# Sparse attention and a gated feed-forward layer on one core: all engines in source order to the end of block one, heads on even and odd partitions, half products in front

## The chip, the core and the metric

The kernel runs on one core of one Trainium2 chip. The metric is the device time of one execution in microseconds (us); less is better. A core has PE (matrix products), DVE (vector work), ACT (activations and copies), POOL (general work) and SP, whose queue issues all of this kernel's transfers. Each engine works through its own queue in order and waits for semaphores of the others.

## What is computed

For 8 batches of 576 tokens and 8 heads of 64, each head attends sparsely: heads 0 to 3 to the last 32 positions, heads 4 to 7 to the earlier positions that agree modulo 32. The 4608 x 512 result goes through a feed-forward layer with 2048 hidden columns.

```python
mask_local = (rel >= 0) & (rel < stride)
mask_strided = (rel >= 0) & (pos[None, :] % stride == pos[:, None] % stride)
...
attn = np.exp(scores)
attn = attn / (np.sum(attn, axis=-1, keepdims=True) + 1e-09)
return np.matmul(attn, v).astype(np.float32)
...
h = x @ w_in
g = h * (1.0 / (1.0 + np.exp(-h)))
return (g @ w_out).astype(np.float32)
```

## The kernel before

**Attention.** A batch is six groups: three local ones of 12 tiles, three strided ones of 8, 8 and 6. A group covers pairs of heads. It runs through these steps:

- scores (L265): the keys of both heads lie block-diagonally in a buffer kbd, and one product per tile gives both heads' scores in a PSUM bank pss
- peaks (L278, DVE, one per part of 64 columns): scores plus mask, and the row's peak
- exp, in two forms. In batch 0 ("early") POOL subtracts the whole group from its peaks (L290), ACT takes one exp (L291), DVE sums (L292). In later batches ACT takes one exp with a sum per part (L284)
- reciprocal of the sum (L295, L296); strided groups are multiplied by it on DVE (L299)
- transposes (L307) and a copy pt (L309); values (L316 local, L336 strided); local results are scaled (L322), transposed back (L328) and copied into xb (L331), strided ones are copied there into strided places (L349)

Loads of kbd and vbd (values) write 64 partitions per transfer, one half of the partitions for each head of a pair (L226 to L237). Three buffers of each serve batch 0, two serve the later batches.

**Feed-forward.** Tokens go in nine blocks of 512, hidden columns in 16 steps of 128. A step is `hidden` (L372: twelve products of 512 columns, three for each of the four 128-row parts of x, because x and the weights are split into a high and a low part), the silu (L393 tanh on ACT, L394 on DVE, L354 high part ghi on DVE, L355 low part glo, on POOL in block one and on DVE later), and `output` (L401, twelve products) one step behind. The x parts xhi and xlo come from L354 (ACT) and L355 (DVE).

**Weights.** The weights are loaded once, in 32 pieces that come as 64-bit numbers through six staging buffers. A piece costs two activations on ACT (L164, L169) and three operations on DVE (L172, L176, L177). `weights(2 * fc + 3)` splits up to piece 2*fc+2 ahead of step fc of block one.

**Order.** `between` runs after each `hidden` and each `output` of a block, 32 times ("halves"), and does the next piece of a later batch's attention at set halves (`due_at`). Only from the first product on, and only on PE, is the order the source's (L534). Everything else, and PE up to there, is ordered by a scheduler that goes by its own times. Loads up to the end of batch 0's attention are chained in the order of `FIRST` (L50: k and v are loads of a group, p of a piece), and the first piece's split is held behind the last exp of batch 0 (`marks`, L512).

Of the kernel before, what the change touches and what calls it, by code (L numbers as in the profile page):

```python
# [17 lines left out]
PSUM = bass.MemoryType.PSUM  # L18

B, H, S, D = 8, 8, 576, 64  # L20
DM, DFF = 512, 2048
STRIDE = 32
# [27 lines left out]
FIRST = "k0 k1 k2 v0 k3 v1 k4 k5 v2 p0 p1 v3 v4 v5 p2 p3 k6 k7 v6 p4 p5"  # L50
# [29 lines left out]
def sparse_attention_ffn(ctx: ExitStack, tc: tile.TileContext, kqt, vt, w_in, w_out, out):  # L80
# [8 lines left out]

    ident = const.tile([P, P], F32, name="ident")  # L90
    make_identity(nc, ident)
# [7 lines left out]
    def keep(m, p0, rows, shape, steps, base, channel):  # L99
# [6 lines left out]


    lent = {
        (1, 0, 12): "stage0", (1, 0, 14): "stage1", (1, 1, 12): "stage2", (1, 1, 14): "stage3",
        (1, 0, 9): "vbd2", (1, 1, 9): "zeros", (1, 0, 7): "kbd2",  # L110
    }

    kbds = [const.tile([P, 3, QW], F32, name=f"kbd{i}") for i in range(KBUFS + 1)]
    vbds = [const.tile([P, 2, VT * D], F32, name=f"vbd{i}") for i in range(VBUFS + 1)]
    zeros = const.tile([P, VT * D], F32, name="zeros")
    nc.vector.memset(zeros, 0.0)
    for kbd in kbds:
        nc.vector.memset(kbd[D:P, 0], 0.0)  # L120
        nc.vector.memset(kbd[0:D, 2], 0.0)
    for vbd in vbds:
        nc.scalar.copy(out=vbd[D:P, 0], in_=zeros[D:P])
        nc.scalar.copy(out=vbd[0:D, 1], in_=zeros[0:D])
    vbds = [vbd.rearrange("p h (t d) -> p h t d", d=D) for vbd in vbds]

# [6 lines left out]
    for starts in sorted({s for g in GROUPS for s in g.starts if s}):  # L133
        first = const.tile([P, 72], F32, name="mask_first" + "".join(map(str, starts)))
        nc.vector.tensor_copy(out=first, in_=m)
        for t in starts:
            keep(first, t * STRIDE, STRIDE, [KW], [1], -STRIDE, 0)
        masks[True, starts] = first
    m = mask("mask_strided")
# [39 lines left out]
    queue = []  # L179
    last = {}  # L180
    marks = []
    ordered = True

    def load(out, in_):

        if not ordered:
            nc.sync.dma_start(out=out, in_=in_)
        elif queue:
            with tc.issue_after(queue[-1]):
                queue.append(nc.sync.dma_start(out=out, in_=in_).ins)  # L190
        else:
            queue.append(nc.sync.dma_start(out=out, in_=in_).ins)
# [33 lines left out]
    def load_qk(b, gi):  # L226
        n = max(GROUPS[gi].nq, GROUPS[gi].nk)
        for h in range(2):
            rows = slice(h * D, (h + 1) * D)
            load(out=kbds[gi % (KBUFS if b else KBUFS + 1)][rows, h : h + 2, :n],  # L230
                 in_=kqt[b, gi, rows, :, :n])

    def load_v(b, gi):
        n = GROUPS[gi].count
        for h in range(2):
            rows = slice(h * KW, (h + 1) * KW)
            load(out=vbds[gi % (VBUFS if b else VBUFS + 1)][rows, h, :n], in_=vt[b, gi, rows, :n])  # L237
# [8 lines left out]
    def attention(gi, b, early):  # L246

        g = GROUPS[gi]

        def bank(name):  # L250

            if early and name != "pss":
# [3 lines left out]
        kbd = kbds[gi % (KBUFS + 1 if early else KBUFS)]  # L256
        vbd = vbds[gi % (VBUFS + 1 if early else VBUFS)]
        cols = g.n * P
        tiles = [(t, t // g.per, slice(t % g.per * g.rows, (t % g.per + 1) * g.rows))
                 for t in range(g.count)]  # L260

        pss = bank("pss")
        s_ps = pss.rearrange("p (c h k) -> p c h k", h=2, k=KW)
        for t, c, rows in tiles:
            nc.tensor.matmul(  # L265
                s_ps[rows, c], kbd[:, 1, g.q0[t] : g.q0[t] + g.rows],
                kbd[:, 0:3:2, g.k0[t] : g.k0[t] + KW], start=True, stop=True,
            )
        yield

        sm = att.tile([P, 512], F32, name="sm")
# [348 lines left out]
```

## Time and profile before

| | us |
|---|---|
| three runs | 983.05, 984.2, 986.59 |
| median | 984.2 |
| the profiled execution | 985.2 |
| its span | 983.4 |
| PE busy in the span | 943.8 |
| PE busy before 76.33 us | 43.2 |

The profile shows one execution. A row of its timeline gives the start, the length, the engine, the line of the kernel, the operation with what it writes and reads, and in brackets how long the engine stood idle before it and what released it. PE's busy time overlaps (the next product starts before the last has drained), so rates are taken from the distance between starts.

### The profile page before, as it was taken

Reading aid. Unit: us, or ns where it says so; the run is one execution under the profiler, and the core shown is the slowest. Engines: PE = TensorE matmul, PEld = TensorE weight load, DVE = VectorE, ACT = ScalarE, POOL = GpSimd, SP = SyncE. Lnnn points to the kernel's source line nnn. Section 1 sums busy time; section 2 is a strip of 40 time slices with the busy share of each in tenths; the row PEclk is TensorE's granted clock in tenths of the full one; section 3 lists DMA queues with packets and bytes.
Section 4 is the critical chain, followed back from the end, with each engine's and each line's share of the span. In section 5 each row is a group of like instructions: output and inputs, shape, how many; then the busy total and the mean of one; then the engine's idle time right before and its main releaser. Section 6 shows DMA issues by size and latency. Waiting matters only on the chain.

```text
span 983.4 us, 15231 instructions
## 1 busy us (share of the span) xinstructions
PE 943.8 (96%) x5896; PEld 749.5 (76%) x5896; DVE 421.1 (43%) x1384; ACT 323.6 (33%) x988; POOL 37.0 (4%) x44
## 2 busy tenths in 40 slices
PE   5559999999999999999999999999999999999998
PEld 3447877778777877787777877787778878888886
DVE  5986733344354334433434344343433333334232
ACT  4865524224242323333423233232422231012011
POOL 3022122000000000000000000000000000000000
PEclk9769999999999999999999999999999999999999
DMA  9974411201131023111211113011210010001001
GB/s 229 279 266 145 147 38 52 90 25 45 50 97 36 26 53 95 44 37 44 77 57 43 44 35 106 26 45 51 86 36 20 1 44 1 1 0 43 1 1 43
DMA packets 36488, 62.86 MB, mean 64 GB/s; under 512 B 4161, under 2 KB 23617, under 8 KB 36417
## 3 DMA queue, kind: packets, MB, share of 16 engines
q1 hardware_dynamic: 36416, 61.90, 21.5%
q8 instruction: 46, 0.75, 0.3%
q14 instruction: 26, 0.20, 0.1%
HBM read 52.45 MB, written 9.44 MB: 63 GB/s over the span
## 4 chain that ended last, share of the span: by engine, by line
PE 91%; DMA 4%; DVE 2%; ACT 1%; POOL 1%; issue 0%; SPq 0%; ACTq 0%; POOLq 0%
PE po L405 41%; PE ps L377 40%; PE ps L265 4%; PE ps L336 2%; DMA stage<-w_out 2%; PE ps L316 2%; PE ps L307 2%; DMA stage<-w_in 1%; POOL glo L355 1%; PE ps L328 1%; DVE stage L172 1%; DMA vbd<-vt 1%; ACT sm L284 0%; ACT stage L164 0%; DMA kbd<-kqt 0%
## 5 line engine op out<-in xcount | busy, mean ns | idle before, releaser
L377 PE MATMUL ps<-xhi,w 128*128 128x512 f32 x1152 | 391.6, 400 | 7.1 <-ACT xhi L354 7.1
L394 DVE SCALAR_TENSOR_TENSOR th<-th,ps 128x512 f32<-128x512 f32 (+1 forms) x147 | 99.3, 676 | 424.4 <-ACT th L393 423.9
L377 PEld LDWEIGHTS ps<-xhi,w 128*128 128x128 f32 x1152 | 217.7, 189 | 63.7 <-ACT xhi L354 7.7
L393 ACT ACTIVATE th<-ps 128x512 f32<-128x512 f32 (+1 forms) x147 | 86.4, 588 | 495.7 <-PE ps L377 491.7
L377 PE MATMUL ps<-xlo,w 128*128 128x512 f32 x576 | 228.2, 396 | 1.3 <-DVE xlo L355 1.3
L405 PE MATMUL po<-w,ghi 128*128 128x512 f32 x576 | 189.8, 401 | 0.7 <-DVE ghi L354 0.7
L405 PEld LDWEIGHTS po<-w,ghi 128*128 128x128 f32 x576 | 107.4, 189 | 28.8 <-issue 4.2
L377 PEld LDWEIGHTS ps<-xlo,w 128*128 128x128 f32 x576 | 109.2, 190 | 26.4 <-DVE xlo L355 2.5
L405 PE MATMUL po<-w,glo 128*128 128x512 f32 x252 | 100.6, 399 | 4.5 <-POOL glo L355 4.5
L284 ACT ACTIVATE sm<-sm,nmax 128x64 f32<-128x64 f32 x280 | 93.8, 337 | 31.2 <-DVE nmax L278 31.2
L355 DVE TENSOR_TENSOR glo<-th,ghi 128x512 fp32r<-128x512 f32 (+1 forms) x131 | 89.0, 679 | 8.9 <-DVE ghi L354 0.5
L405 PE MATMUL po<-stage,ghi 128*128 128x512 f32 x288 | 90.9, 397 | 0.0
L354 DVE CAST ghi<-th 128x512 fp32r<-128x512 f32 (+1 forms) x147 | 61.8, 420 | 9.0 <-DVE th L394 0.5
L405 PEld LDWEIGHTS po<-stage,ghi 128*128 128x128 f32 x288 | 53.6, 188 | 12.7
L405 PEld LDWEIGHTS po<-w,glo 128*128 128x128 f32 x252 | 47.8, 190 | 16.7 <-POOL glo L355 5.4
L405 PE MATMUL po<-stage,glo 128*128 128x512 f32 x144 | 56.8, 395 | 0.0
L265 PE MATMUL ps<-kbd 128*32 128x128 f32 (+1 forms) x928 | 47.7, 289 | 8.5 <-DMA kbd<-kqt 8.5
L284 ACT ACTIVATION_READ_ACCUMULATOR sm<-sm,nmax 128x1 f32 x280 | 52.8, 189 | 0.0
L265 PEld LDWEIGHTS ps<-kbd 128*32 128x32 f32 (+1 forms) x928 | 35.1, 125 | 16.9 <-issue 16.2
L405 PE MATMUL po<-vbd,ghi 128*128 128x512 f32 x108 | 43.9, 407 | 0.0
L405 PE MATMUL po<-vbd,glo 128*128 128x512 f32 x108 | 42.4, 392 | 0.0
L405 PE MATMUL po<-zeros,ghi 128*128 128x512 f32 x108 | 42.1, 390 | 0.0
(75 smaller groups left out, 740.0 us busy)
## 6 DMA issues: line engine op xcount, KB each, us to landing
vbd<-vt SPq DMA_DIRECT2D x48, 192.0 KB, 3.3
out<-osb SPq DMA_DIRECT2D x36, 256.0 KB, 2.1
stage<-w_in SPq DMA_DIRECT2D x16, 512.0 KB, 5.9
stage<-w_out SPq DMA_DIRECT2D x16, 512.0 KB, 4.2
kbd<-kqt SPq DMA_DIRECT2D x32, 221.0 KB, 3.6
kbd<-kqt SPq DMA_DIRECT2D x32, 208.0 KB, 3.4
vbd<-vt SPq DMA_DIRECT2D x32, 128.0 KB, 2.7
kbd<-kqt SPq DMA_DIRECT2D x16, 224.0 KB, 3.6
```

The source lines that it names most:

```text
L172: nc.vector.scalar_tensor_tensor(out=upper, in0=upper, scalar=3, in1=lower, op0=ALU.logical_shift_left, op1=ALU.bitwise_or,)
L265: nc.tensor.matmul(s_ps[rows, c], kbd[:, 1, g.q0[t] : g.q0[t] + g.rows], kbd[:, 0:3:2, g.k0[t] : g.k0[t] + KW], start=True, stop=True,)
L284: last["act"] = nc.scalar.activation(out=s_sb[:, c, h], in_=s_sb[:, c, h], func=AF.Exp, bias=nmax[:, c, h : h + 1], scale=-1.0, accum_out= ...
L307: nc.tensor.transpose(psp[:, at], sm[:, at], ident)
L316: nc.tensor.matmul(o_ps[rows, c], pt[:, c * P + rows.start : c * P + rows.stop], vbd[:, :, t], start=True, stop=True,)
L336: last["pe"] = nc.tensor.matmul(pso[h * D : (h + 1) * D, t * SEQ : (t + 1) * SEQ], vbd[:, h, t], pt[:, p0 : p0 + SEQ], start=True, stop=True,)
L354: copy(out=hi, in_=src)
L355: sub(out=lo, in0=src, in1=hi.bitcast(F32))
L377: nc.tensor.matmul(ph, weight(0, wi, fc)[:, cc * P : (cc + 1) * P], x[xi][:, cc], start=n == 0, stop=n == 3 * NP - 1,)
L393: nc.scalar.activation(out=th[:, cols], in_=ph[:, cols], func=AF.Tanh, scale=0.5)
L394: nc.vector.scalar_tensor_tensor(out=th[:, cols], in0=th[:, cols], scalar=1.0, in1=ph[:, cols], op0=ALU.add, op1=ALU.mult,)
L405: nc.tensor.matmul(po[tt], g[gi][:, cols], weight(1, wi, fc), start=fc == 0 and n == 0, stop=fc == NFC - 1 and n == 2,)
```

## The change

- **Source order.** PE is in source order from the start, and ACT, DVE, POOL and SP are too until block one ends (`others.close()`). The chained loads, `marks` and `issue_after` go. Blocks two to nine are scheduled as before.
- **The prologue written out.** A loop over eight steps s does: peaks of group s, values of s-2, sum and transposes of s-1, scores of s+1, transposes back of s-2. Weight piece 0 is split at s = 5, behind the peaks and the exp of the last group; the high and low parts of x for the first two of its four parts follow at once, and the sum of group 4 comes behind them.
- **Half products.** At s = 6 the products of steps 0 and 1 over the first half of x run, the second of them behind piece 1. Block one's first two steps run only the other half.
- **Even and odd partitions.** The two heads of a pair lie on even and odd partitions in kbd and vbd. A load writes every second partition (`h::2`) instead of 64 in a row. Scores read the keys of both heads in turn (`"p h k -> p k h"`), so in pss and sm the heads alternate by column.
- **Start.** Memsets clear whole buffers, so each first load waits for its buffer's memset; two value buffers are cleared by ACT in four copies.
- **Batch 1 ("quick", b < 2).** Its exp takes batch 0's form, so POOL and DVE have the subtraction and the sum in block one; the strided groups' multiplication is POOL's in both batches. Batch 1's groups come at halves 5, 10, 14, 19, 23, 28 instead of 1, 6, 12, 17, 22, 28, and the next scores and peaks two halves later, instead of three. A group's sum stands one half behind its peaks; for the pairs of halves 0 and 1, 2 and 3, 12 and 13, 16 and 17, 30 and 31 that is within one step, with no piece and no silu between.
- **glo** is DVE's in block one too.

```diff
-FIRST = "k0 k1 k2 v0 k3 v1 k4 k5 v2 p0 p1 v3 v4 v5 p2 p3 k6 k7 v6 p4 p5"
+FIRST = "k0 k1 v0 k2 k3 v1 k4 v2 k5 p0 v3 v4 v5 p1 p2 p3 p4 k6 v6 p5 k7"
...
+    ctx.enter_context(tc.manual_schedule(engines={PE}))
+    others = ctx.enter_context(ExitStack())
+    others.enter_context(tc.manual_schedule(engines=OTHERS))
+    nc.vector.memset(kbds[0][:, 0], 0.0)
+    nc.gpsimd.memset(kbds[0][:, 2], 0.0)
+    nc.vector.memset(kbds[1][:, 0:3:2], 0.0)
+    nc.vector.memset(vbds[0], 0.0)
+    nc.vector.memset(zeros, 0.0)
+    nc.vector.memset(kbds[2][:, 0:3:2], 0.0)
...
-            load(out=kbds[gi % (KBUFS if b else KBUFS + 1)][rows, h : h + 2, :n],
-                 in_=kqt[b, gi, rows, :, :n])
+            load(out=kbds[gi % (KBUFS if b else KBUFS + 1)][h::2, h : h + 2, :n],
+                 in_=kqt[b, gi, h::2, :, :n])
...
-                kbd[:, 0:3:2, g.k0[t] : g.k0[t] + KW], start=True, stop=True,
+                    kbd[:, 0:3:2, g.k0[t] : g.k0[t] + KW].rearrange("p h k -> p k h"),
+                    start=True, stop=True,
...
-            last["dve"] = nc.vector.tensor_mul(s_sb[:, : g.n], s_sb[:, : g.n], inv)
+                (nc.gpsimd if self.quick else nc.vector).tensor_mul(s_sb, s_sb, self.inv)
...
-        sub = nc.vector.tensor_sub if k else nc.gpsimd.tensor_sub
...
+    load_due()
+    scores(0)
+    x = new_x()
+    half_done = {}
+    early = range(NP // 2)
+    late = range(NP // 2, NP)
+    for s in range(NG + 2):
+        if s < NG:
+            groups[s].peak()
+        if s == NG - 1:
+            weights(1)
+            split_x(0, x, early)
+        if 2 <= s:
+            values(s - 2)
+        if 1 <= s <= NG:
+            groups[s - 1].total()
+            groups[s - 1].turn()
+        if s + 1 <= NG:
+            scores(s + 1)
+        if 2 <= s:
+            groups[s - 2].back()
+        if s == NG:
+            half_done[0] = hidden(0, x, early)
+            weights(2)
+            split_x(0, x, [NP // 2])
+            half_done[1] = hidden(1, x, early)
+    split_x(0, x, late[1:])
...
+        plan[at(gi)] += [(groups[c - 1].back if c > NG else None), functools.partial(values, c)]
...
+                plan[then] += [functools.partial(scores, c + n), groups[c + n].peak]
+                plan[then + 1].insert(0, groups[c + n].total)
+    plan[0] += [groups[NG].peak]
+    plan[1] += [groups[NG].total]
...
+            if k == 0 and fc in half_done:
+                ph = hidden(fc, x, late, half_done[fc])
```

ACT's queue in the second half of batch 0's attention; stage is a weight piece's staging buffer, sm and pt are a group's scores and their transposed copy. Before:

```order
L309 COPY pt<-po 128x384
L164 ACTIVATE stage_224<-stage_224 128x512
L169 ACTIVATE stage_224<-stage_224 128x512
L331 COPY xb<-po 128x384
L354 CAST xhi<-xb 128x512
L291 ACTIVATE sm<-sm 128x512
L164 ACTIVATE stage_352<-stage_352 128x512
L169 ACTIVATE stage_352<-stage_352 128x512
L309 COPY pt<-po 128x512
```

And now:

```order
L318 COPY pt<-po 128x384
L362 COPY xb<-po 128x384
L301 ACTIVATE sm<-sm 128x512
L318 COPY pt<-po 128x512
L362 COPY xb<-po 128x384
L301 ACTIVATE sm<-sm 128x384
L174 ACTIVATE stage_242<-stage_242 128x512
L179 ACTIVATE stage_242<-stage_242 128x512
L365 CAST xhi<-xb 128x512 x2
```

The first piece has moved behind the last group's exp, and x's parts behind it.

PE at the end of the first two products' early part, where the last values of batch 0 stand between the halves. Now:

```order
L389 MATMUL ps<-xhi,w_0_423 128x512
L389 MATMUL ps<-xlo,w_0_423 128x512
L389 MATMUL ps<-xhi,w_0_424 128x512
L337 MATMUL po<-pt,vbd_81 64x54 x12
L389 MATMUL ps<-xhi,w_0_423 128x512
L389 MATMUL ps<-xlo,w_0_423 128x512
L389 MATMUL ps<-xhi,w_0_424 128x512
```

Before, at the corresponding place, the last values stood inside the first product alone, and a group of batch 1's values followed soon:

```order
L336 MATMUL po<-pt,vbd_86 64x54 x12
L377 MATMUL ps<-xhi,w_0_580 128x512
L377 MATMUL ps<-xlo,w_0_580 128x512
L377 MATMUL ps<-xhi,w_0_581 128x512
L377 MATMUL ps<-xhi,w_0_580 128x512
L377 MATMUL ps<-xlo,w_0_580 128x512
L377 MATMUL ps<-xhi,w_0_581 128x512
L316 MATMUL ps<-vbd_84,pt 32x128 x12
```

Twelve products, six of each of the two steps, now stand ahead of those values; batch 1's first values have moved behind the second output group.

POOL's last rows; sm<-nmax,sm is the subtraction, sm<-sm,rsum the multiplication. Before:

```order
L290 TENSOR_TENSOR sm<-nmax,sm 128x384 x3
L290 TENSOR_TENSOR sm<-nmax,sm 128x512 x2
L290 TENSOR_TENSOR sm<-nmax,sm 128x384
L355 TENSOR_TENSOR glo<-th,ghi 128x512 x16
L616 UNCONDITIONAL_BRANCH
```

And now, from the multiplication of group 3 on:

```order
L310 TENSOR_TENSOR sm<-sm,rsum 128x4x2x64
L299 TENSOR_TENSOR sm<-nmax,sm 128x3x2x64
L310 TENSOR_TENSOR sm<-sm,rsum 128x4x2x64
L310 TENSOR_TENSOR sm<-sm,rsum 128x3x2x64
L299 TENSOR_TENSOR sm<-nmax,sm 128x3x2x64 x3
L299 TENSOR_TENSOR sm<-nmax,sm 128x4x2x64
L310 TENSOR_TENSOR sm<-sm,rsum 128x4x2x64
L299 TENSOR_TENSOR sm<-nmax,sm 128x4x2x64
L310 TENSOR_TENSOR sm<-sm,rsum 128x4x2x64
L299 TENSOR_TENSOR sm<-nmax,sm 128x3x2x64
```

The sixteen glo are gone, and the subtractions of batch 1 and six multiplications have come.

More of the change, by code (lines that the diff above doesn't have):

```diff
@@ L104, in keep @@
         )
[L108 to L125, printed above, removed]
     masks = {}
@@ L177, in split_weights @@
         nc.vector.tensor_sub(out=lo, in0=value, in1=hi.bitcast(F32))
[L179 to L192, printed above, removed]
+    load = nc.sync.dma_start
     pieces = [(0, 0)]
@@ L498, in sparse_attention_ffn @@
-    work = attention_steps()
-    def attend(groups):
-        while len(weighed) < min(groups, NG * B):
-            next(work)
     ready = 0
```

395 lines of the change are left out of this document (194 added, 201 removed).

## The prediction

> **What bounds the kernel now.** I read the page first, then the windows of PE either side of 76.33 us, the waits of PE behind that point, and last the timeline in front of it. On the page: PE's total, its busy tenths, the clock.
>
> ```profile
> PE 943.8 (96%) x5896; PEld 749.5 (76%) x5896; DVE 421.1 (43%) x1384; ACT 323.6 (33%) x988; POOL 37.0 (4%) x44
> PE   5559999999999999999999999999999999999998
> PEclk9769999999999999999999999999999999999999
> ```
>
> The windows of PE (start:end, length, busy, count, clock, DMA share, GB/s) and its waits after 76 us:
>
> ```profile
> 0.00:76.33 76.33, 43.23 (x456) 0.80 0.87 249
> 76.33:984.00 907.67, 900.58 (x5445) 1.00 0.16 48
> PE po L405 <- POOL glo L355: 1.4, 2, 0.7
> PE po L405 <- DVE ghi L354: 0.6, 1, 0.6
> ```
>
> From 76.33 us on, PE waits 2.0 us in 907 and has its full clock: that part is matmul work, and an order of other engines cannot shorten it by more than those 2.0. In front of it PE is busy 43.2 of 76.3 us at a clock of 0.80. 76.33 is where the second group of output products begins; I use it as the meeting point of both kernels. The timeline in front of it (start, us, engine, line, what; idle before and its releaser):
>
> ```profile
> 5.05 1.51 PE L265 MATMUL ps<-kbd 128*32 128x128 f32 x24 [5.05 <-DMA kbd<-kqt]
> 23.73 0.65 ACT L164 ACTIVATE stage<-stage 128x512 f32<-128x512 f32 x1 [3.06 <-DMA stage<-w_in]
> 27.86 1.09 PE L307 MATMUL po<-ident,sm 128*128 128x128 f32 x4 [6.23 <-DVE sm L299]
> 38.84 1.75 PE L336 MATMUL po<-pt,vbd 128*64 128x54 f32 x32 [4.72 <-ACT pt L309]
> 52.42 0.65 ACT L164 ACTIVATE stage<-stage 128x512 f32<-128x512 f32 x1 [2.46 <-DMA stage<-w_out]
> 54.17 0.79 PE L377 MATMUL ps<-xhi,w 128*128 128x512 f32 x1 [6.38 <-ACT xhi L354]
> 62.58 4.47 POOL L355 TENSOR_TENSOR glo<-th,ghi 128x512 fp32r<-128x512 f32 x1 [31.27 <-DVE ghi L354]
> 67.10 0.80 PE L405 MATMUL po<-w,glo 128*128 128x512 f32 x1 [3.81 <-POOL glo L355]
> 76.33 0.73 PE L405 MATMUL po<-w,ghi 128*128 128x512 f32 x2
> ```
>
> The four long PE waits have one pattern. Weight pieces stand in ACT's and DVE's queues ahead of what PE needs: ACT stops at 20.67 for a piece that lands at 23.7, the attention's copies and the last x parts queue behind, and PE pays 6.23, 4.72 and 6.38 us. The fourth, 3.81, is a 4.47 us subtraction on POOL.
>
> **The change, part by part.** Its own length per step comes from these rows of before.
>
> ```profile
> 6.74 0.23 DVE L278 CUSTOM_DVE_ANT_0 sm<-ps,mask_first 128x64 f32<-128x64 f32 x1 [1.46 <-PE ps L265]
> 7.61 0.08 DVE L278 DVE_READ_ACCUMULATOR2_ANT nmax<- 128x1 f32 x1
> 7.85 0.83 POOL L290 TENSOR_TENSOR sm<-nmax,sm 128x384 f32<-128x384 f32 x1 [2.01 <-DVE nmax L278]
> 8.71 0.52 ACT L291 ACTIVATE sm<-sm 128x384 f32<-128x384 f32 x1 [1.65 <-POOL sm L290]
> 9.72 0.55 PE L307 MATMUL po<-ident,sm 128*128 128x128 f32 x3
> 11.03 0.46 ACT L309 COPY pt<-po 128x384 f32<-128x384 f32 x1
> 14.34 1.28 PE L316 MATMUL po<-vbd,pt 128*32 128x128 f32 x24
> 15.69 0.56 DVE L322 TENSOR_TENSOR xq<-po,rsum 128x384 f32<-128x384 f32 x1 [2.82 <-PE po L316]
> 18.04 1.05 POOL L290 TENSOR_TENSOR sm<-nmax,sm 128x512 f32<-128x512 f32 x1 [4.47 <-DVE rsum L295]
> 20.73 0.68 DVE L292 TENSOR_REDUCE rsum<-sm 128x8 f32<-128x512 f32 x1
> 68.71 0.69 ACT L164 ACTIVATE stage<-stage 128x512 f32<-128x512 f32 x1
> 69.30 0.68 ACT L169 ACTIVATE stage<-stage 128x512 int32<-128x512 uint32 x1
> 71.10 0.63 PE L405 MATMUL po<-w,glo 128*128 128x512 f32 x1
> 71.53 0.68 DVE L177 TENSOR_TENSOR zeros<-stage,vbd 128x512 fp32r<-128x512 f32 x1
> 72.13 0.68 DVE L172 SCALAR_TENSOR_TENSOR stage<-stage 128x512 int32<-128x512 int32 x1
> 72.74 0.41 DVE L176 CAST w<-stage 128x512 fp32r<-128x512 f32 x1
> 71.53 0.63 PE L377 MATMUL ps<-xhi,w 128*128 128x512 f32 x1
> 75.53 0.86 PE L265 MATMUL ps<-kbd 128*32 128x128 f32 x24
> 99.78 0.39 PE L377 MATMUL ps<-xhi,w 128*128 128x512 f32 x1
> 102.57 0.49 PE L328 MATMUL ps<-ident,xq 128*128 128x128 f32 x3
> ```
>
> Read as lengths: a group's peaks 0.95 us for six parts (6.74 to 7.69), 1.25 for eight; subtraction on POOL 0.83 or 1.05; exp 0.52; sum with its two small followers about 1.05; a weight piece 1.15 on ACT (0.59 to the next start and a like second half) and 1.6 on DVE (0.60, 0.61, 0.41); twelve warm 512-column products 2.79 (99.78 to 102.57), cold ones 0.43 each (71.10 to 71.53). A handover between engines costs about 0.1 (7.69 to 7.85 is 0.16, 8.68 to 8.71 is 0.03).
>
> *Stretch A, to the end of batch zero's last scores.* The first loads now wait for a memset of their whole buffer, about 0.7 us, so the first scores start at 5.7 instead of 5.05. No weight piece stands between the groups any more. The first ring takes 4.0 us (peaks 0.95, subtraction 0.83, exp 0.52, transposes 0.55, scores 0.86, handovers 0.3), a later local one 3.2 (peaks 0.95, values 1.28 beside subtraction and exp, transposes 0.55, scores 0.9, less what overlaps): scores end at 7.2, 11.2, 14.4, 17.6. The strided groups close a longer ring: peaks 1.25, subtraction 1.05, the multiplication that moves from DVE to POOL 1.05 (by the subtraction of the same size), transposes 0.55, scores 1.1, handovers and a wait for values 1.3: 6.3. The last scores end near 24. The load of the first piece lies behind some 4.3 MB; at the 249 GB/s of the window row that lands near 20, and it is read only after the last exp, near 26. Piece one stands on SP behind the sixth group's values, whose buffer is free near 18.5; by the same rate it lands near 26 and is read at 37. So the even and odd partitions, whatever they do to a load, save nothing here.
>
> *Stretch B, to the first half product.* Here the change puts work on the path that before had done early: peaks 0.95, subtraction 0.83, exp 0.52, piece zero 1.15 and 1.6, two low parts of x 1.2, then the sum 1.05 that in source order waits behind them, multiplication 1.05, transposes 0.55, scores 1.0, values 1.1, transposes 0.4, nine handovers 0.9: 12.3 us. The half products begin at 36.3; before, the first product's last quarter waited for its x until 54.17.
>
> *Stretch C, to the second output group.* Six cold products 2.6 (38.9); the second six wait for piece one, at about 39.0 by ACT and DVE, and end at 41.6; values 0.9, their copy 0.8, the last x part 1.2 (44.6), and the late half of the first product ends near 45.7. Then the path is: piece two's 1.6 on DVE up to 46.7, the silu's three operations 1.6 (48.3), peaks 0.95, subtraction and exp with handovers 1.65 (50.9), transposes 0.4, scores 0.9 (52.2), output 2.8, product 2.8: 57.8. In source order the next transposes stand ahead of the output group and wait for this exp; that wait, 47.5 to 50.9, is in the sum. The half products themselves save their 12 products of 2.8 us, no more, and only because PE would idle there.
>
> *From there on.* Before needs 983.4 - 76.3 = 907.1 us. Its 2.0 us of waits for ghi and glo go with POOL's subtraction. The order of the products puts one value group, one transposition and one score group later than before: 0.8 (75.53 to 76.33) twice and 0.4 (102.57 and 0.49, less overlap), 2.0 more. New waits: in the first block DVE now has per step two pieces and a silu, 3 x 1.6 = 4.8, against PE's 2 x 2.79 = 5.6; with six groups of 2.4 and five places where its next instruction, the sum, waits for POOL and ACT (1.05 + 0.52 + 0.2 = 1.8), 76.8 + 14.4 + 9 = 100.2 us against PE's 16 x 5.6 + 6 x 2.3 = 103. It fits with little slack; behind DVE's wait stand the pieces for PE's next product. One of the five lies in stretch C; I allow 1.25 us at the other four, 5 us (bounds: 1, and 12 if each of six steps that hold a group slips 2). ACT loses the six or eight separate exps per group and gains nothing there. Later blocks keep their order of products: nothing.
>
> Sum: 57.8 + 907.1 - 2.0 + 2.0 + 5 = 969.9 of span, 13.5 less. The profiled execution took 985.2 us, 1.8 more than its span and 1.0 over the median of 984.2; 984.2 - 13.5 gives 970.7, so **971**. Stretches A and B hold three multiplications on POOL; at 1.05 each as taken, at 4.47 (the longest subtraction above) 7 us more with their neighbours, and with the wait of 12 the own range ends at 981. With shorter handovers, a smooth ring and a wait of 1 it begins at 962.
>
> **The rivals.** *Interleaved keys cost PE.* The scores now read keys of the two heads in turn, elements that lie 896 apart, where before two runs of 64 were read. No row shows PE reading so. For nothing: instructions with 32 rows take 36 ns each (0.86 us for 24), those with 64 rows 68 (1.09 for 16, below), so four of 32 seem to run side by side, each 143 ns for 128 columns, 1.1 ns a column. The 512-column product takes 0.45 (2.79/12/512): one stream reads 2.4 times as fast as scores ask for. Against: on ACT a copy into strided places is dear.
>
> ```profile
> L349 ACT COPY xb<-ps 128x432 f32<-128x432 f32 x7 | 6.7, 963 | 3.6 <-PE ps L336 3.6
> L309 ACT COPY pt<-ps 128x512 f32<-128x512 f32 x14 | 8.2, 583 | 16.1 <-PE ps L307 16.1
> 93.09 1.09 PE L265 MATMUL ps<-kbd 128*64 128x128 f32 x16
> ```
>
> 432 elements take 963 ns where 512 in a row take 583, about twice per element. If scores doubled, as they nearly do at low clock (1.51 against 0.86), a batch would pay 3 x 0.65 + 3 x 0.9 = 4.7 us, and seven batches lie in the part where PE never waits: 33 us, 971 + 33 = 1004. It decides from 1.4 times on, where it eats the 13. I take zero for the sum, by the rate of the 512-column product. The Trainium skill, Advanced Engine Details and Errata, section Memory Cachelines, says that an access needs at least two hits on a 16-byte line of SBUF and pays otherwise; by it each of these reads pays, and the sum would be this rival's. The ACT rows agree; no run here shows it for PE. Chance 0.21.
>
> *POOL and DVE block each other.* The subtraction in the first block stands between DVE's peaks and sum. Before, POOL's glo took these times, against a DVE that worked on:
>
> ```profile
> L355 POOL TENSOR_TENSOR glo<-th,ghi 128x512 fp32r<-128x512 f32 x16 | 26.9, 1680 | 110.3 <-DVE ghi L354 94.5 <-DVE rsum L296 7.4 <-DVE nmax L278 4.5
> ```
>
> The mean is 1.68, the first 4.47. If the subtractions take 4.47 instead of 1.05, four waits grow by 3.4: 971 + 14 = 985, no change. The Trainium skill, SBUF — State Buffer, section Who interferes with whom, has POOL shut out for a whole DVE instruction that reads two SBUF tensors. But here DVE mostly stands still while it waits for POOL, so the chance is 0.09.
>
> **How the numbers follow.** Forecast 0.70, interleaved keys 0.21, blocking 0.09. A measurement of this kernel tells about 0.3% from no change, 3 us. Faster: 0.70 and 0.03 of the blocking, 0.73. Same: 0.05 of the blocking and 0.02 of a small price of the keys, 0.07. Slower: 0.01 and 0.19, 0.20. The forecast's own range is 962 to 981. To hold 8 in 10 the range starts a little lower, at 960, takes in the blocking and the cheaper half of the keys' prices, and ends at 993.
>
> **What would show it.** Right: PE's half products near 36, the second output group near 58, PE waits of about 5 us behind it in the first block, put down to DVE's pieces or ghi; scores of 0.86 and 1.09 as before. Wrong: scores longer than 1.2 us (keys); POOL's subtractions of 3 us and more in the first block; a first piece read later than 28; PE waits in later blocks.

## The result, and the profile after

The changed kernel takes 993.1 us (median of four runs, 992.0 to 994.1), the kernel before 983.6 beside it (four runs, 982.3 to 986.6): a ratio of 1.0092 with a 95% interval of 1.0066 to 1.0118, 9.5 us slower. The profiled execution of the changed kernel took 994.1 us with a span of 992.3. Its page, in the rows that were shown of before:

```profile
PE 952.7 (96%) x5896; PEld 751.2 (76%) x5896; DVE 437.9 (44%) x1396; ACT 311.0 (31%) x912; POOL 22.2 (2%) x43
PE   6589898999999999999999999999999999999998
PEclk9889999999999999999999999999999999999999
```

The second output group now starts at 61.44 us. The windows either side of it (start:end, length, busy, count, clock, DMA share, GB/s), and PE's waits behind it:

```profile
0.00:61.44 61.44, 38.09 (x404) 0.86 0.61 201
61.44:992.30 930.86, 914.58 (x5493) 1.00 0.17 54
PE ps L389 <- DVE w L186: 5.8, 4, 1.9
PE ps L389 <- DVE xlo L366: 2.8, 1, 2.8
PE ps L268 <- DMA kbd<-kqt: 2.7, 2, 2.0
PE po L418 <- DVE ghi L365: 0.3, 1, 0.3
```

So the prologue did what was asked of it: 76.33 became 61.44, 14.9 us less. Everything behind it, 907.1 us before, takes 930.9: 23.8 us more. PE's waits there are 11.6 us where before they were 2.0, and its busy time is 14.0 more (914.6 against 900.6). Some 1.3 of that is work that has moved behind the cut (5493 instructions against 5445): the version R below issues the same 5493 there and is busy 901.9. A good part of the rest is the scores, in all of the later batches. In the timeline (start, us, engine, line, what) a local group and a strided one, each with the product that follows it; first before, then the changed kernel:

```profile
183.60 0.86 PE L265 MATMUL ps<-kbd 128*32 128x128 f32 x24
184.39 0.73 PE L405 MATMUL po<-w,ghi 128*128 128x512 f32 x2
200.18 1.10 PE L265 MATMUL ps<-kbd 128*64 128x128 f32 x16
201.20 0.50 PE L377 MATMUL ps<-xhi,w 128*128 128x512 f32 x1
```

```profile
185.79 1.02 PE L268 MATMUL ps<-kbd 128*32 128x128 f32 x24
186.74 0.74 PE L418 MATMUL po<-w,ghi 128*128 128x512 f32 x2
202.48 1.32 PE L268 MATMUL ps<-kbd 128*64 128x128 f32 x16
203.73 0.51 PE L389 MATMUL ps<-xhi,w 128*128 128x512 f32 x1
```

From start to next start that is 0.79 and then 0.95, 1.02 and then 1.25 us, and for the last strided group, of 12 instructions, 0.81 and 0.97: three, two and one of these a batch make 0.48 + 0.46 + 0.16 = 1.1 us, and seven batches lie behind the second output group: 7.7.

The other part lies in block one. The timeline of the changed kernel at one of its waits, PE's 1.19 us at 101.98, with what DVE, ACT and POOL do ahead of it:

```profile
97.08 1.04 POOL L299 TENSOR_TENSOR sm<-nmax,sm 128x512 f32<-128x512 f32 x1 [20.84 <-PE ps L359]
98.16 0.63 ACT L301 ACTIVATE sm<-sm 128x512 f32<-128x512 f32 x1 [7.31 <-POOL sm L299]
98.70 0.67 ACT L174 ACTIVATE stage<-stage 128x512 f32<-128x512 f32 x1
98.82 0.69 DVE L306 TENSOR_REDUCE rsum<-sm 128x8 f32<-128x512 f32 x1 [1.91 <-ACT sm L301]
99.95 0.69 DVE L182 SCALAR_TENSOR_TENSOR stage<-stage 128x512 int32<-128x512 int32 x1
100.10 1.45 POOL L310 TENSOR_TENSOR sm<-sm,rsum 128x512 f32<-128x512 f32 x1 [1.97 <-DVE rsum L308]
100.68 1.15 DVE L186 CAST w<-stage 128x512 fp32r<-128x512 f32 x1
101.98 0.47 PE L389 MATMUL ps<-xhi,w 128*128 128x512 f32 x1 [1.19 <-DVE w L186]
```

ACT stands 7.31 us at an exp that waits for POOL's subtraction, with two landed weight pieces behind it; DVE stands 1.91 us at the sum that waits for the exp, with the first piece's three steps and the silu behind it. So the piece that PE's next product needs is cast at 100.68, by DVE's wait some 2 us later than it could be.

### The profile page after: what moved, and what is told of

The parts are those of the page before. It is cut to its first block, busy times and chain, and to the rows that moved or that the text cites. A ratio compares the mean times of both kernels' runs of the same rounds, so it can differ in the third digit from the quotient of the medians.

```text
span 992.3 us, 15195 instructions
## 1 busy us (share of the span) xinstructions
PE 952.7 (96%) x5896; PEld 751.2 (76%) x5896; DVE 437.9 (44%) x1396; ACT 311.0 (31%) x912; POOL 22.2 (2%) x43
## 4 chain that ended last, share of the span: by engine, by line
PE 87%; DVE 5%; DMA 3%; ACT 2%; issue 1%; POOL 1%; SPq 0%; POOLq 0%; ACTq 0%; DVEq 0%
PE ps L389 39%; PE po L418 38%; PE ps L268 4%; DMA stage<-w_out 2%; PE ps L337 2%; PE ps L326 2%; PE ps L316 1%; DVE stage L182 1%; DMA stage<-w_in 1%; ACT stage L179 1%; POOL sm L299 1%; PE ps L359 1%; DVE w L186 1%; ACT stage L174 1%; DVE w L187 1%
## 5 line engine op out<-in xcount | busy, mean ns | idle before, releaser
L366 DVE TENSOR_TENSOR glo<-th,ghi 128x512 fp32r<-128x512 f32 (+1 forms) x147 | 100.1, 681 | 10.5 <-DVE ghi L365 0.9
L292 ACT ACTIVATE sm<-sm,nmax 128x64 f32<-128x64 f32 x240 | 81.0, 341 | 38.1 <-DVE nmax L285 38.1
L268 PE MATMUL ps<-kbd 128*32 128x128 f32 (+1 forms) x928 | 56.9, 321 | 8.8 <-POOL mask_strided L126 5.5
L268 PEld LDWEIGHTS ps<-kbd 128*32 128x32 f32 (+1 forms) x928 | 40.9, 127 | 17.9 <-issue 9.2
L292 ACT ACTIVATION_READ_ACCUMULATOR sm<-sm,nmax 128x1 f32 x240 | 45.0, 187 | 0.0
```

What stands on the lines that cost most here:

```text
L268: nc.tensor.matmul(s_ps[rows, c], kbd[:, 1, g.q0[t] : g.q0[t] + g.rows], kbd[:, 0:3:2, g.k0[t] : g.k0[t] + KW].rearrange("p h k -> p k h") ...
L292: nc.scalar.activation(out=s_sb[:, c, h], in_=s_sb[:, c, h], func=AF.Exp, bias=nmax[:, c, h : h + 1], scale=-1.0, accum_out=rsum[:, c, h : ...
L366: sub(out=lo, in0=src, in1=hi.bitcast(F32))
```

## The experiments

My theory: two losses of their own, the interleaved keys (7.7 us) and the source order in block one (the 11.6 us of waits and what a stop costs PE beside them), stand against the prologue's 14.9. The main rivals: that the waits set the pace, so that shorter scores give nothing back, and that they come from the work moved into block one or from late transfers, whatever the order. In the diffs "..." stands for lines left out. An added line of code shifts the numbers, so that L268 of the changed kernel is L269 or more in some runs. In the table a row's parts are those of its profiled execution, with the start of the second output group as the cut; ratios are to the kernel before, run beside it.

| kernel | second output group | behind it | median us | ratio, 95% interval |
|---|---|---|---|---|
| before | 76.33 | 907.1 | 983.6 | |
| changed | 61.44 | 930.9 | 993.1 | 1.0092, 1.0066 to 1.0118 |
| keys in runs | 64.35 | 925.4 | 990.3 | 1.0058, 1.0044 to 1.0073 |
| before, keys in turn | 72.90 | 915.9 | 992.6 | 1.0083, 1.0065 to 1.0101 |
| block one scheduled | 78.40 | 917.1 | 998.0 | 1.0137, 1.0119 to 1.0155 |
| both | 84.94 | 907.9 | 993.9 | 1.0096, 1.0080 to 1.0112 |
| exp and sum later | 62.77 | 927.1 | 991.0 | 1.0063, 1.0046 to 1.0080 |
| keys in runs, exp and sum later | 64.23 | 920.9 | 988.0 | 1.0038, 1.0019 to 1.0056 |
| scheduled, pieces held | 62.79 | 914.3 | 978.9 | 0.9941, 0.9927 to 0.9956 |
| R: keys in runs, scheduled, held | 62.77 | 906.4 | 971.1 | 0.9867, 0.9852 to 0.9883 |
| SP alone scheduled | 60.98 | 928.7 | 992.9 | 1.0089, 1.0068 to 1.0109 |
| all but SP scheduled, held | 63.53 | 914.4 | 979.8 | 0.9952, 0.9935 to 0.9969 |
| DVE alone scheduled, held | 56.55 | 921.8 | 981.5 | 0.9968, 0.9953 to 0.9982 |
| ACT alone scheduled, held | 65.16 | 927.5 | 994.3 | 1.0088, 1.0058 to 1.0118 |
| whole products in the changed kernel | 56.98 | 931.7 | 990.0 | 1.0045, 1.0030 to 1.0061 |
| R with whole products | 55.64 | 907.1 | 964.7 | 0.9805, 0.9787 to 0.9822 |
| R with the first half product alone | 58.69 | 907.2 | 968.1 | 0.9827, 0.9798 to 0.9855 |
| R with keys on partition halves | 64.39 | 907.5 | 971.6 | 0.9872, 0.9851 to 0.9893 |

**The keys.** First the reading alone, put into the kernel before (masks and values keep their order, so this kernel does not compute the attention; the work is the same):

```
-                s_ps[rows, c], kbd[:, 1, g.q0[t] : g.q0[t] + g.rows],
-                kbd[:, 0:3:2, g.k0[t] : g.k0[t] + KW], start=True, stop=True,
+                pss[rows, c * P : (c + 1) * P].rearrange("p (k h) -> p k h", h=2), kbd[:, 1, g.q0[t] : g.q0[t] + g.rows],
+                kbd[:, 0:3:2, g.k0[t] : g.k0[t] + KW].rearrange("p h k -> p k h"),
+                start=True, stop=True,
```

> The kernel before with one thing alone: the scores' product reads the two heads' keys in turn, as the changed kernel does, and writes them in that order; masks, sums and values are left as they were, so a column of the scores stands for another key than the values behind it take. Work and order are the same. Theory (the interleaved reading has a price on PE, 1.1 us a batch): 983.6 rises to 991 to 992, scores 0.86 to 1.02 us and 1.09 to 1.32. Rival (it has no price of its own, and the longer scores of the changed kernel come from what runs beside them in its order, or from the partitions that the keys were loaded to): 983 to 984.5, scores of 0.86 and 1.09 us.

Measured: 992.6 beside 984.8 of the kernel before, 7.8 us more. In the stretch from 300 to 980 us, where both kernels issue the same 620 score instructions that the trace holds, the scores alone were busy (first before, then with keys in turn):

```profile
300.00:980.00 680.00, 62.75 (x620) 1.00 0.13 38
```

```profile
300.00:980.00 680.00, 68.10 (x620) 1.00 0.13 38
```

5.4 us more in 5.3 batches (a batch has 116 such instructions), 1.0 a batch in busy time, close to the 1.1 from start to start in the changed kernel. The results are written in the same places as before, so the price is the reading's own. The counterpart takes it out of the changed kernel:

```
-            load(out=vbds[gi % (VBUFS if b else VBUFS + 1)][h::2, h, :n], in_=vt[b, gi, h::2, :n])
+            rows = slice(h * KW, (h + 1) * KW)
+            load(out=vbds[gi % (VBUFS if b else VBUFS + 1)][rows, h, :n], in_=vt[b, gi, rows, :n])
...
-            s_ps = self.pss.rearrange("p (c k h) -> p c k h", h=2, k=KW)
+            s_ps = self.pss.rearrange("p (c h k) -> p c h k", h=2, k=KW)
...
-                    kbd[:, 0:3:2, g.k0[t] : g.k0[t] + KW].rearrange("p h k -> p k h"),
+                    kbd[:, 0:3:2, g.k0[t] : g.k0[t] + KW],
...
```

> The changed kernel with the keys of a pair's heads back in two runs of 64: the scores' moving operand, the bank of scores and their copy go back to the order part, head, key, and the values' rows follow; the loads of the keys keep even and odd partitions, and all orders stay. In the trace of the changed kernel the scores' instructions got longer than before (24 in a local group from 0.79 to 0.95 us from start to next start, 16 in a strided one from 1.02 to 1.25, 12 from 0.81 to 0.97), 1.1 us a batch. Theory (the interleaved reading costs PE, in seven batches behind the second output group about 7.7 us): 993.1 falls to about 985, with scores of 0.86 and 1.09 us again and the same 11.6 us of PE waits. Rival (the waits of block one set the pace and take up whatever the scores give back): no change, 991 to 994.

Measured: 990.3, only 2.8 off where 8 were expected; between theory and rival. Behind the second output group 5.5 us went. The scores are short again, but the waits stay (11.7 us), and in the profiled run PE's clock fell in two more stretches behind them. First the changed kernel, then this run:

```profile
120.00:128.00 8.00, 7.61 (x41) 1.00 0.04 8
144.00:152.00 8.00, 6.60 (x28) 1.00 0.21 73
```

```profile
120.00:128.00 8.00, 6.80 (x22) 0.79 0.00 0
144.00:152.00 8.00, 6.40 (x41) 0.79 0.50 143
```

With 13.2 us of busy time at 0.79, the two stretches cost some 2.8 us. The prologue was 2.9 later at a clock of 0.81 instead of 0.86; whether that came from the values' loads or from where the clock fell isn't settled by this run. (In the scheduled pair below, which differs by the same edit, the second output group comes at 62.79 and 62.77.) What settles the keys' price in the changed order is the pair of scheduled versions below.

**Source order in block one.** The plain test ends the source order one block sooner:

```
     split_x(0, x, late[1:])
+    others.close()
...
-        if k == 0:
-            others.close()
```

> The changed kernel with the source order of ACT, DVE, POOL and SP ended one block sooner, ahead of the first block's first whole step; the prologue and its half products stay in source order. Theory (in source order the pieces on DVE and ACT queue behind instructions that wait for POOL's subtraction and for transfers, and PE pays 11.6 us behind the second output group where before paid 2.0): PE's waits behind 61.4 us fall to about 2 to 4, the time to about 984. Rival (the waits come from the work that the change moves into that block, exps in one piece with their subtraction on POOL and the low part of the silu on DVE, in whatever order it is issued): 992 to 995 with 10 us of waits.

> Both edits together: keys in two runs of 64 again, and ACT, DVE, POOL and SP ordered by the scheduler from the first block on. Theory (interleaved reading and source order in block one are two separate losses, 8 and 8 to 9 us, beside the 15 us that the prologue gains): about 976, which is below both kernels. Rival (one of the two is no cause): 984 to 985; (neither is): 993.

Both missed on the total (998.0 and 993.9) and came as the theory said behind the cut: 917.1, which is 13.8 less than the changed kernel, and with the keys in runs 907.9, close to the 907.1 of before. But the scheduler now drew weight pieces into the prologue, as in the kernel before. From the first of the two runs:

```profile
PE po L316 <- POOL sm L310: 15.1, 2, 12.2
```

A sum's followers stand on DVE between pieces, the multiplication on POOL comes late, PE waits 12.2 us for it, and the cut moves to 78.40. So these runs left a rival standing: that block one was smooth only because the pieces were done early.

Next, source order kept, but the steps that wait written later (in the prologue the exp still follows its peaks at once):

```
                 nc.gpsimd.tensor_sub(s_sb[:, : g.n], peak, s_sb[:, : g.n])
+
+        def power(self):
+            if self.quick:
                 sm = self.sm[:, : self.cols]
                 nc.scalar.activation(out=sm, in_=sm, func=AF.Exp)
...
-                plan[then + 1].insert(0, groups[c + n].total)
+                wait = 2 if b == 1 else 1
+                plan[then + 1].insert(0, groups[c + n].power)
+                plan[then + wait].insert(wait == 1, groups[c + n].total)
```

> The changed kernel with two steps of the next batch's softmax written later in block one: the exp, which waits for POOL's subtraction, one half step behind the peaks, and the sum, which waits for the exp, another half step later. All engines stay in source order to the end of block one. Theory (ACT and DVE stand still at exp and sum, 32.7 and 7.0 us in all, with the next weight pieces queued behind them, and PE pays for it): PE's waits for DVE's w behind the second output group fall from 5.8 to under 2 us and the time from 993 to 988 or less. Rival (the pieces are late because their transfers are, which are queued behind other loads on SP): 992 to 994, w waits of 5 us and more.

> Keys in two runs of 64 again, and exp and sum half a step and a whole step later in block one, all engines in source order. Theory (two separate losses): 980 to 983, the interleaved keys' 7.7 and the waits' 5; rival (with shorter scores PE comes sooner to the same late pieces): 987 to 990.

Measured: 991.0 and 988.0; the theory's times were missed by 3 and 5 us. Its mechanism showed in part. PE's waits behind the cut in the first of the two:

```profile
PE ps L319 <- POOL sm L313: 3.3, 1, 3.3
PE ps L392 <- DVE xlo L369: 2.6, 1, 2.6
PE ps L392 <- DVE w L186: 1.4, 1, 1.4
PE ps L268 <- DMA kbd<-kqt: 0.7, 1, 0.7
```

The waits for pieces fell from 5.8 to 1.4 as expected, and a new one took part of their place: a sum that comes later makes POOL's multiplication later, and the transposes on PE wait 3.3 us for that.

Then block one scheduled with the pieces held, so that none is drawn into the prologue. `marks` holds the instructions behind which pieces are kept: first the last split of x, then each step's tanh on ACT and low part on DVE.

```
-            split_piece(ready)
+            with ExitStack() as hold:
+                for ins in marks[max(0, len(marks) - 2)] if marks else ():
+                    hold.enter_context(tc.issue_after(ins))
+                split_piece(ready)
...
     split_x(0, x, late[1:])
+    marks.append(list(last))
+    others.close()
...
             new = (k, fc, silu(k, fc, ph))
+            if k == 0:
+                marks.append([tanhs[-1], last[1]])
```

> The changed kernel with ACT, DVE, POOL and SP handed to the scheduler at the start of block one, but unlike the earlier run of this kind the weight pieces are held: none starts ahead of the prologue's last split of x, and those of a step none ahead of the silu two steps before. Theory (the earlier run lost 17 us ahead of the second output group to pieces that were pulled into the prologue, and gained 13.8 behind it): the second output group begins at 61 to 63 us and what follows it takes 917 to 920, together 980 to 984. Rival (the gain behind it came only because the pieces were done early, in the time that the prologue lost): 992 to 998.

> Keys in two runs of 64 again, and block one scheduled with held weight pieces. Theory: 61 to 64 us up to the second output group, and 908 to 911 behind it: 971 to 976, below both kernels. Rival (block one's pace is set by the work of DVE and ACT or by the transfers, whatever the order): 984 and more.

Measured: 978.9 and 971.1, below both kernels, as the theory said, and at or a little under its lower bounds. Neither trace lists a PE wait behind the second output group. The windows of the second:

```profile
0.00:62.77 62.77, 37.94 (x405) 0.84 0.73 212
62.77:969.00 906.23, 901.90 (x5493) 1.00 0.18 55
```

The pair also gives the keys' price clean of waits: 914.3 - 906.4 = 7.9 us, against 7.7 from the rows. And it gives that of source order: 930.9 - 914.3 = 16.6, of which the waits are 11.6. The clock, 0.98 between 100 and 180 us, makes 1.4 to 1.6 of the rest. More goes with each stop: the product at 101.98 above starts 1.59 us behind the one before it instead of 0.23, and it and the next three take 1.20 us instead of 0.93, together 1.63 us lost where a wait of 1.19 is listed. Four stops for pieces, at some 0.4 each, would make 1.6 (an estimate); about 2 us are not put down to anything.

Whose order? First SP against the other three:

```
-    others.enter_context(tc.manual_schedule(engines=OTHERS))
+    others.enter_context(tc.manual_schedule(engines=OTHERS - {mybir.EngineType.SP}))
+    loads = ctx.enter_context(ExitStack())
+    loads.enter_context(tc.manual_schedule(engines={mybir.EngineType.SP}))
...
     split_x(0, x, late[1:])
+    loads.close()
```

> The changed kernel with SP alone given to the scheduler from the start of block one; ACT, DVE and POOL stay in source order to its end. Theory (what PE pays in block one comes from ACT and DVE standing still with other work behind them): no more than 2 us off, 990 to 994. Rival (loads queue behind one another on SP in source order, and late pieces and keys are the cause): about the 979 of the run in which all four are scheduled, PE waits behind the second output group under 2 us.

> The counterpart: ACT, DVE and POOL scheduled from the start of block one with held weight pieces, SP in source order to its end, with the same sequence of loads as in the changed kernel. Theory: 979 to 982, no waits of over 2 us behind the second output group. Rival (SP's order is the cause): 988 to 993, with waits for pieces and keys.

992.9 and 979.8: the order of the loads is no part of it. Then DVE and ACT, one at a time, with the freed engine's part of the weight pieces held:

```
+    freed = {mybir.EngineType.DVE}
+    loads = ctx.enter_context(ExitStack())
+    loads.enter_context(tc.manual_schedule(engines=OTHERS - freed))
     others = ctx.enter_context(ExitStack())
-    others.enter_context(tc.manual_schedule(engines=OTHERS))
+    others.enter_context(tc.manual_schedule(engines=freed))
...
```

> The changed kernel with DVE alone scheduled in block one, its part of the weight pieces held as before; ACT, POOL and SP in source order. Theory (DVE's order is what PE pays for: the sums wait on DVE with pieces behind them): 979 to 983. Rival (ACT's order: exps wait for POOL with pieces and tanh behind them, and DVE only passes it on): 988 to 993.

> The counterpart: ACT alone scheduled in block one, DVE, POOL and SP in source order. Theory (DVE's order): 988 to 993. Rival (ACT's order): 979 to 983. If both are needed, neither run gets below 985.

DVE alone: 981.5 against 993.1; ACT alone: 994.3, no gain (3.4 us less behind the cut, 3.7 more ahead of it). The first also ended a wait of 4.39 us ahead of the cut, for an exp on ACT, and its cut is 4.9 us sooner. Behind the cut it gains 9.1 of the 16.6: 4.2 us of waits are left, 2.0 for keys, 1.9 for x and 0.3 for pieces, where the changed kernel has 5.8 for pieces. POOL alone was not freed. What the scheduler does with DVE, at a strided group's sum in that run:

```profile
86.39 1.08 POOL L302 TENSOR_TENSOR sm<-nmax,sm 128x512 f32<-128x512 f32 x1 [16.70 <-DVE nmax L288]
86.59 1.42 DVE L370 TENSOR_TENSOR glo<-th,ghi 128x512 fp32r<-128x512 f32 x1
87.50 0.63 ACT L304 ACTIVATE sm<-sm 128x512 f32<-128x512 f32 x1 [3.14 <-POOL sm L302]
88.17 0.69 DVE L309 TENSOR_REDUCE rsum<-sm 128x8 f32<-128x512 f32 x1 [0.15 <-ACT sm L304]
```

The rest of the silu stands between peaks and sum, and DVE waits 0.15 us where it waited 1.91. ACT waits for POOL there as well, and PE's timeline has no stop. But between 60 and 170 us all of DVE's waits at sums fall only from 5.4 to 3.7 us, so these rows show one place and not the whole of the gain.

**The half products.** They were undone in the best version so far, both and then the second alone, and in the changed kernel (both):

```
-            half_done[0] = hidden(0, x, early)
...
-            half_done[1] = hidden(1, x, early)
```

> The best version so far (keys in runs, block one scheduled with held pieces, 971.1) without the half products: the first two first products are whole, behind all four parts of x. Theory of the prediction (the half products save their twelve products of 2.8 us, and only because PE would idle there): 973.5 to 975. Rival (the first silu waits in the queues of DVE and ACT rather than for PE, so that they save nothing): 970.5 to 972.

> The scheduled version with keys in runs, keeping the first half product and undoing only the second, the one that waits for weight piece one. Theory (only the second stands in the way; the first runs where PE idles): 963.5 to 965. Rival (any half product is a loss, by its place ahead of the last values): 967 to 971.

> The changed kernel with only the half products undone: the first two products are whole, all else as in the changed kernel, interleaved keys and source order too. Theory (the second half product stands on PE ahead of the last group's values and waits for weight piece one, so values, the last parts of x and the first silu come late; that is lost wherever it happens): the second output group 4 to 7 us sooner, 54 to 58, and 986 to 989. Rival (in source order block one's pace is set by DVE and ACT, so that what the prologue gains is given back as waits): 991 to 993.

Without them: 964.7, 6.4 us better, the best of all runs; with the first alone 968.1. Both my theory for the pair (2.5 to 4 worse without) and its rival (no difference) were wrong, and of the two halves each seems to cost about 3. The timelines show two different reasons. First with both halves, then without:

```profile
42.99 0.50 PE L391 MATMUL ps<-xhi,w 128*128 128x512 f32 x1 [2.42 <-DVE w L186]
44.84 0.91 PE L338 MATMUL po<-pt,vbd 128*64 128x54 f32 x24
45.80 0.72 ACT L351 COPY xb<-po 128x306 f32<-128x306 f32 x1 [3.55 <-PE po L338]
55.15 0.90 PE L423 MATMUL po<-w,ghi 128*128 128x512 f32 x2 [3.95 <-DVE ghi L368]
```

```profile
39.88 0.91 PE L338 MATMUL po<-pt,vbd 128*64 128x54 f32 x24 [1.35 <-ACT pt L319]
41.37 0.74 ACT L351 COPY xb<-po 128x306 f32<-128x306 f32 x1
49.23 0.73 PE L423 MATMUL po<-w,ghi 128*128 128x512 f32 x2 [0.34 <-DVE ghi L368]
```

The second half product waits 2.42 us for weight piece one, and in PE's order the last values of batch 0 stand behind it: 44.84 instead of 39.88. ACT's copy waits 3.55 us for them, it and the last part of x come 4.4 later, and the first output group 5.9.

The first half product delays none of this: with it alone the first output group begins at 49.21, without it at 49.23, for in both PE waits until 43.5 us for the low part of x, and what was done early is spent waiting. Its 3 us arise behind that, in the order that the scheduler then gives DVE. With the first half product alone, glo comes behind the next group's peaks and beside POOL's subtraction; PE waits for it, and the products after it run at a lower clock. The second of the windows is that of the version without:

```profile
50.53 1.32 DVE L368 TENSOR_TENSOR glo<-th,ghi 128x512 fp32r<-128x512 f32 x1
51.91 0.51 PE L423 MATMUL po<-w,glo 128*128 128x512 f32 x1 [1.97 <-DVE glo L368]
52.00:56.00 4.00, 4.00 (x12) 0.62 0.83 278
52.00:56.00 4.00, 4.00 (x19) 1.00 0.72 248
```

Without it that wait is 0.47. The later glo and the clock make 1.5 us each, the 3.05 by which the second output group comes later. So the first half product gains nothing, and what it costs here may be this schedule's and not its own.

In the changed kernel the edit moves the second output group from 61.44 to 56.98, in the range of the theory (54 to 58), but the time only from 993.1 to 990.0 (by the ratios 4.6 us), between the theory's 986 to 989 and the rival's 991 to 993: source order gives 0.8 us of it back behind the cut, where the waits for pieces are 6.4 now.

**Even and odd partitions.**

```
-            load(out=kbds[gi % (KBUFS if b else KBUFS + 1)][h::2, h : h + 2, :n],
-                 in_=kqt[b, gi, h::2, :, :n])
+            rows = slice(h * D, (h + 1) * D)
+            load(out=kbds[gi % (KBUFS if b else KBUFS + 1)][rows, h : h + 2, :n],
+                 in_=kqt[b, gi, rows, :, :n])
...
```

> The same best version with the keys' and queries' rows back on the two halves of the partitions, as values already are there, so that nothing is left of even and odd partitions. Theory of the prediction (they save nothing that the path sees): 970 to 972.5. Rival (loads of every other partition land sooner, 3.1 instead of 3.4 to 3.6 us, and the prologue is short of loads): first scores and the second output group 1 to 3 us later, 972.5 to 975.

971.6 against 971.1: within what the intervals leave, no difference. The rival's premise did show, the time did not: most loads of keys took 3.5 to 3.6 us to land instead of 3.0, the first scores began at 5.79 instead of 5.33, and the second output group came 1.6 us later, in a profiled execution that was the longest of the four (973.9).

## Why the prediction was wrong

It said 971 and faster; the kernel is slower, at 993.1. Two terms of the sum failed. One is the price of the interleaved keys, "I take zero for the sum": it is 7.9. The other is the 5 us of new waits in block one: the waits alone are 11.6, and source order costs 16.6 with what goes with them. The span was to be 969.9 and is 992.3, 22.4 more: 7.9 for the keys, 11.6 for source order (the 16.6 less the 5 allowed), 3.6 up to the second output group (1.3 by the end of stretch B, the rest in stretch C), and 0.7 less for the work behind the cut (906.4 instead of 907.1, in the version that has neither of the two).

- *Stretch A* held: the last scores end at 24.3 us (24), the first piece is read without a wait at 26.9, POOL's subtractions take 0.83 and 1.05 on the mean.
- *Stretch B*: 36.3 was said, the half products begin at 37.57. The transposes ahead of them wait 6.69 us for POOL's multiplication, as its ring of steps said.
- *Stretch C*: 57.8 was said, 61.44 came. Two pieces of its working fail: the second half product, to begin when piece one is there "at about 39.0", began at 40.99, and its delay goes on into the values and x; and transposes, scores and the first output products run at a lower clock (0.50 between 52 and 56 us; 1.51 us for scores taken at 0.9).

```profile
33.45 1.12 PE L316 MATMUL po<-ident,sm 128*128 128x128 f32 x4 [6.69 <-POOL sm L310]
37.57 0.48 PE L389 MATMUL ps<-xhi,w 128*128 128x512 f32 x1
40.99 0.50 PE L389 MATMUL ps<-xhi,w 128*128 128x512 f32 x1 [1.77 <-DVE w L186]
52.48 0.90 PE L316 MATMUL ps<-ident,sm 128*128 128x128 f32 x3 [4.39 <-ACT sm L301]
53.31 1.51 PE L268 MATMUL ps<-kbd 128*32 128x128 f32 x24
```

- *The half products* were said to "save their 12 products of 2.8 us" because PE would idle there. They cost: 6.4 us in the scheduled version, 3.1 in the changed kernel. For the second of them, the sentence looked at PE's idle time and not at what stands behind it on PE: the wait for piece one was in the sum, its price for the values and x was not. For the first, what PE saves it waits for x afterwards.
- *Interleaved keys* were a rival at 0.21, doubled scores, 33 us, 1004. The rival was true and its size wrong: 1.2 times, 1.1 us a batch, below the 1.4 from which it was to decide alone. It took over half of the 13.5 us that were forecast as gain, and source order more than the rest. The argument for zero was that a 512-column product takes 0.45 ns a column where the scores take 1.1. Both rates are of keys or x read in a run, and say nothing on reading in turn. The second argument, ACT's copies into strided places, pointed the right way. The Trainium skill, Advanced Engine Details and Errata, section Memory Cachelines, asks for two hits on a line: by it the reads in turn pay, and they do; the size, 0.16 to 0.23 us a group, is from these runs.
- *New waits*: place and cause were named, DVE's sum waiting for POOL and ACT with the pieces behind it. They were priced by filling DVE to 100.2 of 103 us, and each slip at 1.25. At that filling there was no room to catch up: PE stopped four times for pieces alone, 5.8 us, and for the last split of x and for keys 5.5 more. That DVE's order is a cause is shown by freeing DVE alone: 11.6 us of the time, and 9.1 of the 16.6 behind the cut. The rest goes only when ACT and POOL are free too; which of the two, and by which way the slips came to keys and x, was not followed.
- *POOL and DVE block each other*, 0.09: the subtractions between peaks and sum do not lengthen. Beside POOL's multiplication DVE's cast does, 1.15 us instead of 0.43 (in the rows at 100 us above): 0.7 us of that wait, not the 3.4 each of the rival.
- *Even and odd partitions*: "save nothing here" held.

With the keys in runs and DVE free, the sum's own structure comes true: 62.8 and 906.4 us, 971.1.

## What to carry to other kernels

A queue in source order is as good as the place of its waiting instructions: ahead of every wait, write the work that needs nothing from it, and read behind every wait who stands there. Early work on an idle engine is free only if nothing urgent is queued behind it, and only if its own inputs have landed: the second half product held up the last values. And it saves only what the engine doesn't spend waiting afterwards: the first saved nothing. A layout that helps one stage is paid in every later batch: price it by one run of the kernel before with the new access and nothing else.

## What the runs showed of the hardware

Products whose moving operand takes the keys of two heads in turn, 896 elements apart, took 1.2 times as long (0.79 to 0.95, 1.02 to 1.25, 0.81 to 0.97 us), while DVE's peaks and ACT's exps over every second element stayed as they were: 220 and 221 ns, 337 and 341 ns (before, then the changed kernel). DVE's low part of the silu took 1.42 us beside POOL's subtraction (at 86.59 above), where its mean is 0.68, and 1.32 at 50.53 in the version with the first half product alone. The Trainium skill, SBUF — State Buffer, section Who interferes with whom, lets a DVE instruction with two inputs in SBUF contend with POOL's reads, and one of the two then stands; these rows agree. Beside DVE's cast at 100.68 both were longer, the cast 1.15 for 0.43 and POOL's multiplication 1.45 where the other three of its size took 1.04 to 1.05. After PE's wait of 2.77 us at 169.06 in the changed kernel the granted clock was low: from 170.0 to 173.0 the products stood 0.43 us apart instead of 0.23, which is 1.4 us of work, half of what the wait itself cost:

```profile
168.00:172.00 4.00, 2.94 (x8) 0.71 0.01 2
172.00:176.00 4.00, 4.00 (x16) 0.87 0.06 22
```
